# Sixteen chained score matmuls per head pair undone, and the last tile's 32-row stores on ScalarE's queue (block-sorted attention followed by a residual MLP, one core)

## The chip, the cores and the metric

One NeuronCore of a Trainium2 chip runs the whole program. The metric is the device time of one execution in microseconds (us). Beside it stands the span, from the first to the last instruction that the hardware profiler recorded. PE is TensorE, ACT ScalarE, DVE VectorE, POOL GpSimd, SP SyncE, which here only issues DMAs and waits.

## The reference, cut to what matters

```python
# sort_net (4, 8, 8, 8) -> P: five rounds of exp and normalising, one 8x8 matrix per batch and head
k_sorted = einsum('bhij,bhjcd->bhicd', P, k_blocks)      # 8 blocks of 96 tokens, 64 wide
v_sorted = einsum('bhij,bhjcd->bhicd', P, v_blocks)
scores = matmul(q_block, k_sorted_block.T) / sqrt(64)    # 96 x 96 in each block
attn = exp(scores - max); attn = attn / sum(attn)
x = matmul(attn, v_sorted)                               # 4 batches of 768 tokens x 512

# the residual MLP on x
a1 = alpha1 * x + beta1
u = x + lam * einsum('ts,bsd->btd', w_tok, a1)           # mixes tokens, 768 x 768
a2 = alpha2 * u + beta2
out = u + lam * (maximum(a2 @ w_ch1, 0) @ w_ch2)         # 512 -> 2048 -> 512
```

Inputs and output are float32; the matmuls run on fp16 and bf16 copies.

## The kernel before

Four batches go through the same stages. Per batch: the 8x8 matrices are spread to 128x128 (`mixing_matrices`, L267), V and K are mixed by blocks (`mix_v`, `mix_k`), the attention runs by head pairs (`emit_attention`, L512), and the MLP follows: `moe_a` (token mixing `tok_ps`, the sum u, its transposition), `moe_h` (L666, 512 to 2048 with Relu: `h_ps`) and `moe_ch` (L680, 2048 to 512: `ch_ps`, then two DVE operations, then the stores). The MLP of batch b-1 is written beside the attention of batch b, so that PE has `h_ps` and `ch_ps` matmuls to do while the attention waits for its exponentials.

**The attention of batches 1 to 3.** A head pair h4 (two heads on partitions 0 to 63 and 64 to 127, four pairs) has 8 blocks in two groups g of four. A group takes eight score matmuls (K = 64 rows, 96 x 96 each; the two heads alternate between the two halves of the rows), one exponential on ACT over 96 x 768 values (`et`), eight `x_ps` matmuls (96 rows, 65 columns wide: values and row sums) and, on DVE, a reciprocal and one or two multiplications into x (`x128`; `xs` for the blocks 6 and 7, which `gather` copies to the last 32 partitions afterwards). `emit_attention` asks for the scores of pair h4 ahead of the `x_ps` of pair h4-1.

**Buffers.** `sc_ps`, `x_ps`, `k_ps`, `v_ps` and `rep_ps` take turns in the pool psA with two buffers of two PSUM banks. In the steady state a buffer goes scores of pair h4+1, `x_ps` of pair h4, scores of pair h4+2: the scores are released by their exponential, the `x_ps` by the last DVE multiplication that reads it. `h_ps`, `ch_ps` and `tok_ps` use psB with four banks.

**The order.** Up to the loop of L792 the instructions of each engine keep their written order (`keep_in_program_order`, the flag `fixed`; from L766 to L791 it is taken off and put on by engine). In the loop over batches 1 to 3 the order on each engine is fixed at compile time by a planner: it takes the written order as priority, estimates what each instruction costs, and where the first in line is not yet ready by its estimate it puts a later one. On the chip each engine then runs its list in order, and an instruction that waits holds up what stands behind it.

**The chain of sixteen.** `emit_pair` (L432) draws both psA buffers of a pair, lets the first score wait for everything in `freed[b]` (the last instructions that empty a psA buffer or fill kT: the last `mix_k` copies, the last exponential or the last DVE multiplication), and ties each of the other fifteen scores behind the one before, so that the planner puts sixteen in a row. Batch 0 uses `emit_scores`, eight at a time, in a written order.

**The stores.** For each tile of 128 rows of the result `moe_ch` issues two DMAs on SP's queue, one for 96 rows (L695) and one for 32 rows of the tail (L696). The last tile of the last batch is worked in two column ranges, 384 and 128 wide, with two stores each.

Of the kernel before, what the change touches and what calls it, by code (L numbers as in the profile page):

```python
# [7 lines left out]
FT = mybir.dt.float32  # L8
# [8 lines left out]
def kernel(  # L17
# [20 lines left out]
    nc = tc.nc  # L38

    B, H, S, D = q.shape  # L40
    NB = sort_net.shape[-1]
    BLK = S // NB
# [9 lines left out]
    TAIL = 6 * BLK  # L52
# [20 lines left out]
    pe = Engine(nc.tensor)  # L73
    dve = Engine(nc.vector)
    act = Engine(nc.scalar)
# [9 lines left out]
    def psa(shape, dtype, name):  # L85
        return psA.tile(shape, dtype, name=name, tag="psA")

    def psb(shape, dtype, name):
        return psB.tile(shape, dtype, name=name, tag="psB")

    def const(shape, dtype, name):
# [5 lines left out]
        out=ident16[:], in_=ident16[:], compare_op=ALU.not_equal, fill=1.0, base=0,  # L97
# [31 lines left out]
    qT_of = {}  # L129
# [84 lines left out]
    def spin(ps, n):  # L214
        src = ident16[:].unsqueeze(1).to_broadcast([128, 4, 128])
        for _ in range(n):
            pe.matmul(ps, ident16[:], src, start=True, stop=True)
# [104 lines left out]
    kT_of = {}  # L322
# [30 lines left out]
    def mix_k(b, share=(4, 0, 4), gs=range(3)):  # L353
        raw = raw_of[(b, 0)]
        rhs = bigP[b][:].rearrange("p g i -> p (g i)")
        if b not in kT_of:
            kT_of[b] = att.tile([128, H4 * NB, BLK], F16, name="kT", tag="kT", bufs=2)
        kv_ = kT_of[b][:].rearrange("p c (par th tp) -> p th c par tp", th=2, par=2)
        for g in gs:
            kps = psa([128, 8, 128], FT, "k_ps")  # L360
            copies = []
            for tp in range(8):
                t0 = (8 * g + tp) * 128
                pe.matmul(kps[:, tp, :], raw[:, t0:t0 + 128], rhs, start=True, stop=True)
            for par in range(2):
                for h2 in range(2):
                    src = kps[par * 64:(par + 1) * 64, :, h2 * 64:(h2 + 1) * 64].rearrange(
                        "p n (th c) -> p th c n", th=2
                    )
                    dst = kv_[h2 * 64:(h2 + 1) * 64, :, :, par, 8 * g:8 * g + 8]  # L370
                    if 2 * par + h2 < share[g]:
                        ins = dve.tensor_copy(dst, src)
                    else:
                        ins = act.copy(dst, src)
                    copies.append(ins)
            freed[b] = copies

    def mix_heads(kv, h4, out, copies):

# [32 lines left out]

    x_of = {}

    def score(b, h4, blocks, sps):
        for ii, i in enumerate(blocks):
            for h2 in range(2):
                rows = slice(h2 * 64, (h2 + 1) * 64)
                yield pe.matmul(
                    sps[0:BLK, h2, ii, 0:BLK], kT_of[b][rows, h4 * NB + i, :],  # L420
                    qT_of[b][rows, h4, :, i * 16:(i + 1) * 16], start=True, stop=True,
                )

    freed = {}

    def behind(ins, others, kind):
        for other in others:
            tc.add_manual_dep(
                ins.ins, other.ins.name, mybir.DependencyInfo(kind, mybir.DependencyReason.DATA), reason="scores"
            )  # L430

    def emit_pair(b, h4):  # L432

        pair = [psa([128, 2, 4, 128], FT, "sc_ps") for _ in range(2)]
        last = None
        for g in range(2):
            for ins in score(b, h4, range(4 * g, 4 * g + 4), pair[g]):
                if last is None:
                    behind(ins, freed[b], mybir.DependencyClass.Sync)
                else:  # L440
                    behind(ins, (last,), mybir.DependencyClass.NoSync)
                last = ins
        return [emit_exp(ps, b) for ps in pair]

    def emit_scores(b, h4, g, spins=0):
        sps = psa([128, 2, 4, 128], FT, "sc_ps")
        spin(sps[:, 0, :, :].rearrange("p i x -> p (i x)"), spins)
        for _ in score(b, h4, ((0, 1, 2, 6), (3, 4, 5, 7))[g], sps):
            pass
        return emit_exp(sps)  # L450

    def emit_exp(sps, b=0):
        et = att.tile([BLK, 2, 4, BLK], F16, name="et", tag="et", bufs=4)
        freed[b] = [act.activation(
            et[:].rearrange("p a i (r kt) -> p (a i) r kt", kt=NT),
            sps[0:BLK].rearrange("p a i x -> p (a i) x")[:, :, 0:BLK].rearrange("p n (kt r) -> p n r kt", kt=NT),
            AF.Exp, scale=scale,
        )]
        return et

    def emit_pv(b, h4, ets, x128, xs):
        for g in range(2):
            xall = psa([128, 4, 256], FT, "x_ps")
            xps = xall[0:BLK]
            flat = ets[g][:].rearrange("p a i x -> p (a i x)")
            for ii in range(4):
                i = 4 * g + ii
                for h2 in range(2):
                    at = (h2 * 4 + ii) * BLK
                    rows = min(128, 8 * BLK - at)  # L470
                    pe.matmul(
                        xall[0:rows, ii, h2 * GRP:h2 * GRP + D + 1], flat[:, at:at + rows],
                        Vs[b % NV][:, (2 * h4 + h2) * NB + i, 0:D + 1],
                        start=True, stop=True,
                    )
            recip = att.tile([BLK, 4, 2], FT, name="recip", tag="recip", bufs=3)
            sums = xps[:, :, D:D + GRP + 1:GRP]
            vals = xps[:, :, 0:2 * GRP].rearrange("p i (a g) -> p i a g", a=2)[:, :, :, 0:D]
            dve.reciprocal(recip[:], sums)
            for lo, hi in ((0, 4),) if g == 0 else ((0, 2), (2, 4)):  # L480
                i = 4 * g + lo
                cols = slice(h4 * 128, (h4 + 1) * 128)
                dst = x128[0:BLK, i:i + hi - lo, cols] if i < 6 else xs[:, :, cols]
                freed[b] = [dve.tensor_tensor(
                    dst.rearrange("p i (a d) -> p i a d", d=D), vals[:, lo:hi],
                    recip[:, lo:hi].unsqueeze(3).to_broadcast([BLK, hi - lo, 2, D]), ALU.mult,
                )]

    def pv_tiles(h4, g, et, spins=0):

# [21 lines left out]
    def emit_attention(b):  # L512
        x128 = moep.tile([128, NT, C], F16, name="x128", tag="x128", bufs=2)
        xs = moep.tile([BLK, 2, C], F16, name="xs", tag="xs", bufs=1)
        x_of[b] = x128

        def gather(lo, hi):
            for a in range(3):
                dve.tensor_copy(x128[96:128, a:a + 4:3, lo:hi], xs[32 * a:32 * a + 32, :, lo:hi])

        prev = emit_pair(b, 0)
        for h4 in range(1, H4):
            cur = emit_pair(b, h4)
            emit_pv(b, h4 - 1, prev, x128, xs)
            prev = cur
            if h4 == H4 - 1:
                gather(0, 384)
        emit_pv(b, H4 - 1, prev, x128, xs)
        gather(384, C)
# [150 lines left out]
    def moe_ch(b, hf, kks=range(3)):  # L680
        hT = hT_of[(b, hf)]
        for kk in kks:
            kt = 3 * hf + kk
            last = b == B - 1 and kt == NT - 1
            ost = att.tile([128, C], FT, name="ost", tag="ost", bufs=2)
            for lo, hi in ((0, 384), (384, C)) if last else ((0, C),):
                cps = psb([128, hi - lo], FT, "ch_ps")
                for m in range(HT):
                    pe.matmul(
                        cps[:], hT[m][:, kk * 128:(kk + 1) * 128], W2p[:, m, lo:hi],  # L690
                        start=(m == 0), stop=(m == HT - 1),
                    )
                dve.tensor_tensor(cps[:], cps[:], lamB[:, lo:hi], ALU.mult)
                dve.tensor_tensor(ost[:, lo:hi], cps[:], u_of[b][kt][:, lo:hi], ALU.add)
                nc.sync.dma_start(out[b, kt * 96:(kt + 1) * 96, lo:hi], ost[0:96, lo:hi])  # L695
                nc.sync.dma_start(out[b, TAIL + kt * 32:TAIL + (kt + 1) * 32, lo:hi], ost[96:128, lo:hi])  # L696


    ets = {}
# [1 line left out]
    def sc0(h4, g, spins=0):  # L701
        ets[(h4, g)] = emit_scores(0, h4, g, spins)
# [83 lines left out]
    for kk in range(2):  # L786
        moe_ch(0, 0, (kk,))
        mix_k(1, gs=((0, 1), (2,))[kk])
        for h4 in range(2 * kk, 2 * kk + 2):
            turn_q(1, h4, dve.tensor_copy)  # L790
# [59 lines left out]
```

The softmax here doesn't subtract the row's maximum and nothing guards it: scores larger than these inputs give would overflow.

## Time and profile before

| what | us |
|---|---|
| median of 4 runs (lowest to highest) | 269.84 (269.34 to 272.49) |
| the profiled execution | 269.8 |
| its span | 268.0 |
| PE busy | 255.9 (95% of the span) |
| DVE busy | 155.7 (58%) |
| ACT busy | 126.2 (47%) |
| POOL busy | 92.5 (35%) |
| first and last score matmul of the kernel | 18.0 and 196.1 |
| exponential, 96 x 768, each of 32 | 0.806 |
| granted TensorE clock | 1.00 |

In a line of the timeline the first number is the start in us from the beginning of the span, the second the time until the last instruction of the group ends; then engine, line, operation, out<-in, shape, and xN, the number of instructions merged. A matmul's length there is its latency: matmuls overlap, so their rate is read from start to start. L65 is the line of the helper through which the four compute engines issue everything, so groups are told apart by their tiles. SPq lines are DMA issues. A bracket at the end gives the idle time of the engine before the group and what ended it.

### The profile page before, as it was taken

What the parts mean: (1) busy time and instruction counts of PE and PEld (TensorE: products, weight loads), DVE (VectorE), ACT (ScalarE), POOL (GpSimd) and SP (SyncE); (2) the same over time, 40 slices, a digit from 0 to 9 for tenths busy, and PEclk for the clock granted to TensorE, in tenths of its full rate; (3) what the DMA queues carried; (4) which work ended last, traced back from release to release, by engine and by line L of the source; (5) the groups of instructions that cost most, each with busy time, mean ns of one, the idle gap of its engine ahead of it and who ended that gap; (6) DMA issues with size and microseconds to landing.
All of it is one profiled execution on the core that took longest, in us unless ns stands there. A gap on an engine that the chain in (4) does not pass through costs nothing.

```text
span 268.0 us, 5145 instructions
## 1 busy us (share of the span) xinstructions
PE 255.9 (95%) x2048; PEld 141.3 (53%) x2059; DVE 155.7 (58%) x333; ACT 126.2 (47%) x232; POOL 92.5 (35%) x100
## 2 busy tenths in 40 slices
PE   7799999999998999999999999999999999999993
PEld 2467745565555444654565444554565445545542
DVE  5878678629648996712765966714567962042033
ACT  3376757643576131990266313980465305505600
POOL 8523689203682804209527225002407200000000
PEclk9999999999999999999999999999999999999999
DMA  6999999989999443699998343494200332012012
GB/s 79 186 208 245 207 211 206 209 207 109 194 177 160 90 80 100 157 105 102 203 194 105 61 89 90 117 91 68 71 11 2 79 78 78 2 39 78 2 39 78
DMA packets 62423, 30.88 MB, mean 115 GB/s; under 512 B 48888, under 2 KB 58112, under 8 KB 62400
## 3 DMA queue, kind: packets, MB, share of 16 engines
q0 software_dynamic: 23024, 15.60, 39.3%
q1 hardware_dynamic: 39376, 14.96, 33.7%
q8 instruction: 16, 0.26, 0.4%
q14 instruction: 7, 0.06, 0.1%
HBM read 32.78 MB, written 8.65 MB: 155 GB/s over the span
## 4 chain that ended last, share of the span: by engine, by line
PE 73%; DMA 9%; ACT 6%; DVE 5%; POOL 3%; issue 2%; POOLq 0%; ACTq 0%; DVEq 0%
PE ch_ps L65 30%; PE h_ps L65 25%; PE tok_ps L65 9%; DMA wt<-in_moe_w_tok_dram 6%; ACT et L65 3%; DMA W1p<-in_moe_w_ch_dram 3%; PE x_ps L65 3%; DVE x L65 2%; ACT kT L65 2%; PE v_ps L65 2%; PE k_ps L65 1%; PE sc_ps L65 1%; POOL qn L65 1%; POOL raw L65 1%; DVE kT L65 1%
## 5 line engine op out<-in xcount | busy, mean ns | idle before, releaser
L65 PE MATMUL h_ps<-a2T,W1p 128*128 128x384 bf16 x512 | 91.9, 326 | 0.1
L65 ACT ACTIVATE hTa<-h_ps 128x384 bf16<-128x384 f32 x96 | 45.9, 492 | 50.2 <-PE h_ps L65 49.6
L65 PE MATMUL ch_ps<-W2p,hTa 128*128 128x512 bf16 (+2 forms) x289 | 65.7, 370 | 0.6
L65 PEld LDWEIGHTS <-W1p 128*128 128x128 bf16 x512 | 47.8, 98 | 30.7 <-issue 0.6
L65 DVE TENSOR_TENSOR ch_ps<-ch_ps,lamB 128x512 f32<-128x512 f32 (+2 forms) x25 | 16.9, 676 | 62.7 <-PE ch_ps L65 60.1
L65 POOL TENSOR_SCALAR u<-b1lB,rs 128x512 f32<-128x512 f32 x18 | 28.5, 1595 | 65.4 <-DVE ost L65 57.4
L65 PEld LDWEIGHTS <-hTa 128*128 128x128 bf16 x300 | 28.7, 98 | 32.4
L65 ACT ACTIVATE et<-sc_ps 96x768 f16<-96x768 f32 x32 | 24.5, 807 | 22.4 <-PE sc_ps L65 22.4
L65 PE MATMUL tok_ps<-x,w_tokT 128*128 128x512 f16 x144 | 32.3, 379 | 1.0 <-DVE x L65 1.0
L65 POOL TENSOR_TENSOR u<-x,u 128x512 f32<-128x512 f16 x22 | 25.4, 1184 | 21.5 <-DVE x L65 20.7
L65 ACT CAST u<-u 128x512 f16<-128x512 f32 x24 | 14.8, 618 | 26.4 <-DVE u L65 26.4
L65 PE MATMUL ch_ps<-W2p,hTb 128*128 128x512 bf16 (+2 forms) x100 | 25.0, 371 | 0.0
L65 PEld LDWEIGHTS <-w_tokT 128*128 128x128 f16 x180 | 14.7, 97 | 17.2 <-issue 1.0
L65 DVE TENSOR_TENSOR tok_ps<-tok_ps,a1lB 128x512 f32<-128x512 f32 x24 | 16.5, 691 | 4.8 <-PE tok_ps L65 4.7
L65 DVE CAST kT<-k_ps 64x512 f16<-64x512 f32 x24 | 16.5, 688 | 3.3 <-PE k_ps L65 3.0
L65 DVE TENSOR_TENSOR x<-x_ps,recip 96x512 f16<-96x512 f32 (+2 forms) x32 | 17.6, 554 | 1.0
L65 DVE TENSOR_TENSOR u<-tok_ps,u 128x512 f32<-128x512 f32 x24 | 16.4, 688 | 1.7
L65 ACT ACTIVATE hTb<-h_ps 128x384 bf16<-128x384 f32 x32 | 15.3, 499 | 4.1 <-PE h_ps L65 3.7
L65 DVE TENSOR_TENSOR ost<-ch_ps,u 128x512 f32<-128x512 f32 (+2 forms) x25 | 16.6, 666 | 0.7
L65 POOL DMA_DIRECT2D qn<-in_q_dram x18 | 15.4, 875 | 4.2 <-PE q_ps L65 3.4
L65 PEld LDWEIGHTS <-et 96*128 96x128 f16 (+2 forms) x288 | 13.0, 99 | 7.1 <-issue 3.5
L65 PE MATMUL x_ps<-Vs,et 96*128 96x65 f16 (+2 forms) x288 | 14.7, 194 | 1.0 <-ACT et L65 0.8
(95 smaller groups left out, 207.5 us busy)
## 6 DMA issues: line engine op xcount, KB each, us to landing
out_dram<-ost SPq DMA_DIRECT2D x23, 192.0 KB, 2.2
raw<-in_v_dram POOLq DMA_DIRECT2D x8, 384.0 KB, 8.8
raw<-in_k_dram POOLq DMA_DIRECT2D x8, 384.0 KB, 11.0
vscr<-vA SPq DMA_DIRECT2D x6, 384.0 KB, 4.4
Vs<-vscr SPq DMA_DIRECT2D x6, 384.0 KB, 7.5
W1p<-in_moe_w_ch_dram POOLq DMA_DIRECT2D x4, 512.0 KB, 10.6
W2p<-in_moe_w_ch_dram POOLq DMA_DIRECT2D x4, 512.0 KB, 18.2
qn<-in_q_dram POOLq DMA_DIRECT2D x12, 128.0 KB, 5.0
```

What stands on the lines that cost most here:

```text
L65: ins = getattr(self.eng, name)(*args, **kwargs)
```

## The change

The chain of sixteen goes: `emit_pair`, `score`, `behind`, `emit_exp` and the record `freed` are taken out, and `emit_scores`, one group of eight, serves all four batches. Each group's scores then depend only on their operands and on their own psA buffer. The number of matmuls, exponentials and DVE operations stays. For the last tile the two 32-row stores are issued on ScalarE's queue in place of SyncE's.

```diff
@@ mix_k
-            copies = []
...
                     if 2 * par + h2 < share[g]:
-                        ins = dve.tensor_copy(dst, src)
+                        dve.tensor_copy(dst, src)
                     else:
-                        ins = act.copy(dst, src)
-                    copies.append(ins)
-            freed[b] = copies
@@ scores
-    def emit_pair(b, h4):
-
-        pair = [psa([128, 2, 4, 128], FT, "sc_ps") for _ in range(2)]
-        last = None
-        for g in range(2):
-            for ins in score(b, h4, range(4 * g, 4 * g + 4), pair[g]):
-                if last is None:
-                    behind(ins, freed[b], mybir.DependencyClass.Sync)
-                else:
-                    behind(ins, (last,), mybir.DependencyClass.NoSync)
-                last = ins
-        return [emit_exp(ps, b) for ps in pair]
...
+    def emit_scores(b, h4, g, spins=0):
+        kT = kT_of[b]
+        qT = qT_of[b]
+        blocks = ((0, 1, 2, 6), (3, 4, 5, 7))[g] if b == 0 else range(4 * g, 4 * g + 4)
+        sps = psa([128, 2, 4, 128], FT, "sc_ps")
+        spin(sps[:, 0, :, :].rearrange("p i x -> p (i x)"), spins)
         for ii, i in enumerate(blocks):
             for h2 in range(2):
                 rows = slice(h2 * 64, (h2 + 1) * 64)
-                yield pe.matmul(
-                    sps[0:BLK, h2, ii, 0:BLK], kT_of[b][rows, h4 * NB + i, :],
-                    qT_of[b][rows, h4, :, i * 16:(i + 1) * 16], start=True, stop=True,
-                )
+                pe.matmul(
+                    sps[0:BLK, h2, ii, 0:BLK], kT[rows, h4 * NB + i, :], qT[rows, h4, :, i * 16:(i + 1) * 16],
+                    start=True, stop=True,
+                )
         et = att.tile([BLK, 2, 4, BLK], F16, name="et", tag="et", bufs=4)
...
@@ emit_attention
-        prev = emit_pair(b, 0)
+        prev = [emit_scores(b, 0, g) for g in range(2)]
         for h4 in range(1, H4):
-            cur = emit_pair(b, h4)
+            cur = [emit_scores(b, h4, g) for g in range(2)]
             emit_pv(b, h4 - 1, prev, x128, xs)
@@ moe_ch
                 nc.sync.dma_start(out[b, kt * 96:(kt + 1) * 96, lo:hi], ost[0:96, lo:hi])
-                nc.sync.dma_start(out[b, TAIL + kt * 32:TAIL + (kt + 1) * 32, lo:hi], ost[96:128, lo:hi])
+                (nc.scalar if last else nc.sync).dma_start(
+                    out[b, TAIL + kt * 32:TAIL + (kt + 1) * 32, lo:hi], ost[96:128, lo:hi]
+                )
```

More of the change, by code (lines that the diff above doesn't have):

```diff
@@ L371, in mix_k @@
                     if 2 * par + h2 < share[g]:
-                        ins = dve.tensor_copy(dst, src)
+                        dve.tensor_copy(dst, src)
                     else:
-                        ins = act.copy(dst, src)
-                    copies.append(ins)
-            freed[b] = copies
+                        act.copy(dst, src)
     def mix_heads(kv, h4, out, copies):
@@ L413 @@
     x_of = {}
-    def score(b, h4, blocks, sps):
+    def emit_scores(b, h4, g, spins=0):
[4 more added lines that the diff above has]
+        spin(sps[:, 0, :, :].rearrange("p i x -> p (i x)"), spins)
         for ii, i in enumerate(blocks):
@@ L418, in score @@
                 rows = slice(h2 * 64, (h2 + 1) * 64)
-                yield pe.matmul(
-                    sps[0:BLK, h2, ii, 0:BLK], kT_of[b][rows, h4 * NB + i, :],
-                    qT_of[b][rows, h4, :, i * 16:(i + 1) * 16], start=True, stop=True,
-                )
[L424 to L429, printed above, removed]
-            )
-    def emit_pair(b, h4):
-        pair = [psa([128, 2, 4, 128], FT, "sc_ps") for _ in range(2)]
-        last = None
-        for g in range(2):
-            for ins in score(b, h4, range(4 * g, 4 * g + 4), pair[g]):
-                if last is None:
-                    behind(ins, freed[b], mybir.DependencyClass.Sync)
-                else:
-                    behind(ins, (last,), mybir.DependencyClass.NoSync)
-                last = ins
-        return [emit_exp(ps, b) for ps in pair]
[L445 to L452, printed above, removed]
+                pe.matmul(
+                    sps[0:BLK, h2, ii, 0:BLK], kT[rows, h4 * NB + i, :], qT[rows, h4, :, i * 16:(i + 1) * 16],
+                    start=True, stop=True,
+                )
         et = att.tile([BLK, 2, 4, BLK], F16, name="et", tag="et", bufs=4)
-        freed[b] = [act.activation(
+        act.activation(
             et[:].rearrange("p a i (r kt) -> p (a i) r kt", kt=NT),
@@ L457, in emit_exp @@
             AF.Exp, scale=scale,
-        )]
+        )
         return et
@@ L483, in emit_pv @@
                 dst = x128[0:BLK, i:i + hi - lo, cols] if i < 6 else xs[:, :, cols]
-                freed[b] = [dve.tensor_tensor(
+                dve.tensor_tensor(
                     dst.rearrange("p i (a d) -> p i a d", d=D), vals[:, lo:hi],
                     recip[:, lo:hi].unsqueeze(3).to_broadcast([BLK, hi - lo, 2, D]), ALU.mult,
-                )]
+                )
     def pv_tiles(h4, g, et, spins=0):
@@ L695, in moe_ch @@
                 nc.sync.dma_start(out[b, kt * 96:(kt + 1) * 96, lo:hi], ost[0:96, lo:hi])
-                nc.sync.dma_start(out[b, TAIL + kt * 32:TAIL + (kt + 1) * 32, lo:hi], ost[96:128, lo:hi])
+                (nc.scalar if last else nc.sync).dma_start(
+                    out[b, TAIL + kt * 32:TAIL + (kt + 1) * 32, lo:hi], ost[96:128, lo:hi]
+                )
     ets = {}
```

## The prediction

> **What bounds the kernel now.** I read the page's first section, then the timeline of TensorE (PE) through the three attention stages, then the timeline of all engines at the end of the span, then the DMA issues.
>
> ```profile
> span 268.0 us, 5145 instructions
> PE 255.9 (95%) x2048; PEld 141.3 (53%) x2059; DVE 155.7 (58%) x333; ACT 126.2 (47%) x232; POOL 92.5 (35%) x100
> ```
>
> PE is busy for 95% of the span, and from 41 us to 264 us its timeline has hardly a gap: whatever the change does to the time in the middle, it does by adding or removing time in PE's own queue, which runs in order. The granted clock is 1.00 in all the stretches I asked for, so no term below comes from the clock.
>
> The change touches batches 1 to 3. Their attention is woven by the planner between the MLP matmuls of the batch before (h_ps, ch_ps). This is PE in batch 3; the columns are start, length, what, count.
>
> ```profile
> 189.80 2.12 PE L65 MATMUL h_ps<-a2T,W1p 128*128 128x384 bf16 x12
> 191.85 0.56 PE L65 MATMUL sc_ps<-qT,kT 64*96 64x96 f16 x16
> 192.34 0.66 PE L65 MATMUL h_ps<-a2T,W1p 128*128 128x384 bf16 x3
> 193.19 0.41 PE L65 MATMUL x_ps<-Vs,et 96*128 96x65 f16 x8 [0.19 <-ACT et L65]
> 193.44 0.49 PE L65 MATMUL h_ps<-a2T,W1p 128*128 128x384 bf16 x2
> 193.89 0.42 PE L65 MATMUL x_ps<-Vs,et 96*128 96x65 f16 x8
> 194.14 1.63 PE L65 MATMUL h_ps<-a2T,W1p 128*128 128x384 bf16 x9
> 195.70 0.56 PE L65 MATMUL sc_ps<-qT,kT 64*96 64x96 f16 x16
> ```
>
> Four numbers come out of it. (1) An h_ps matmul takes 0.163 us from start to start: two rows not shown here, h_ps x25 at 199.81 and tok_ps at 203.88, give 4.07/25. (2) Scores have a price for coming and going. Twelve h_ps from 189.80 would let the next one start at 191.75; the scores start at 191.85: 0.10 us on entry. Sixteen scores last 0.56 us, of which 0.205 is one matmul's own length (the groups by tile), so they are (0.56-0.205)/15 = 0.024 us apart, 16 make 0.38; the next h_ps starts 0.49 us after the first score: 0.11 us on exit. A visit of sixteen is thus 0.59 us, one of eight 0.10+0.19+0.11 = 0.40 us. (3) The x_ps matmuls cost no such entry: after h_ps x3 at 197.99 they start at 198.48, just 3 x 0.163 later. (4) The two x_ps groups wait for their exponentials: h_ps x3 from 192.34 end their turn at 192.83, x_ps starts at 193.19 (0.36 us lost), and the next, 193.89 against 193.77, loses 0.12. Together 0.48 us a pair; the same spacing stands at 76 to 78, 80 to 81, 132 to 133, 137 and 197 us, so six pairs. The score run itself waits for no buffer there (195.70 is 9 x 0.163 + 0.10 after 194.14, within 0.01).
>
> The second pair of each batch (h4=1) waits for both exponentials of the first:
>
> ```profile
> 175.97 1.31 PE L65 MATMUL h_ps<-a2T,W1p 128*128 128x384 bf16 x7
> 177.46 0.56 PE L65 MATMUL sc_ps<-qT,kT 64*96 64x96 f16 x16 [0.18 <-ACT et L65]
> 177.94 1.15 PE L65 MATMUL h_ps<-a2T,W1p 128*128 128x384 bf16 x6
> ```
>
> Seven h_ps end their turn at 177.11 and the scores start at 177.46: 0.35 us, entry included.
>
> Batch 1 ends differently from 2 and 3, because its filler runs out:
>
> ```profile
> 83.45 2.28 PE L65 MATMUL h_ps<-a2T,W1p 128*128 128x384 bf16 x13
> 85.66 0.20 PE L65 MATMUL rep_ps<-P,ebh 32*128 32x64 f16 x1
> 86.12 0.62 PE L65 MATMUL tok_ps<-x,w_tokT 128*128 128x512 f16 x2 [0.26 <-DVE x L65]
> 87.50 7.50 PE L65 MATMUL tok_ps<-x,w_tokT 128*128 128x512 f16 x34 [0.76 <-DVE x L65]
> 94.84 2.75 PE L65 MATMUL ch_ps<-W2p,hTa 128*128 128x512 bf16 x11
> ```
>
> The thirteen h_ps end their turn at 85.57. Until tok_ps starts at 86.12 PE does one small matmul (0.13 us by its row at 163.59): 0.42 us lost. The 36 tok_ps take 94.84-86.12 = 8.72 us where 36 x 0.216 = 7.77 would do (0.216 from the batch 3 rows, 7.77 us for 36): 0.95 us lost, waiting for the last copies of x by VectorE (DVE). So 1.37 us of PE stand idle. In batches 2 and 3, 34 and 25 h_ps stand between the last x_ps and tok_ps, and nothing is lost.
>
> The end of the span:
>
> ```profile
> 264.13 0.32 SPq L695 DMA_DIRECT2D out_dram<-ost  x1
> 264.34 0.29 DVE L65 TENSOR_TENSOR ost<-ch_ps,u 128x128 f32<-128x128 f32 x1
> 264.50 0.42 SPq L696 DMA_DIRECT2D out_dram<-ost  x1
> 265.01 0.38 SPq L695 DMA_DIRECT2D out_dram<-ost  x1
> 265.44 0.43 SPq L696 DMA_DIRECT2D out_dram<-ost  x1
> ```
>
> ```profile
> out_dram<-ost SPq DMA_DIRECT2D x2, 48.0 KB, 1.7
> out_dram<-ost SPq DMA_DIRECT2D x1, 16.0 KB, 1.5
> ```
>
> The last addition ends at 264.63. SyncE (SP) is then still issuing the first columns' 32-row store until 264.92, and the last store is issued at 265.44; with 1.5 us to landing it lands at 266.94, and 1.1 us of closing work follow.
>
> **The change part by part.** The base is the profiled execution: a span of 268.0 us and 1.8 us around it, taken as unchanged, 269.8 in all; the median of the runs is 269.84, the same.
>
> *The tail.* The stores of the 32 rows go to ScalarE (ACT), which has had nothing since the last h_ps was evicted some 10 us earlier and has nothing behind them. SP then has one issue of 0.32 us, free at 264.45, so both last stores are issued when the sum is ready, near 264.68. With 1.7 us for the 48 KB store it lands at 266.38 in place of 266.94: -0.55 us. The trace has no store issued by ACT. Its bounds: at best the end follows the last issue, which moves from 265.44 to 264.68, -0.76; if it takes the 2.2 us of the big output stores, it lands at 266.88, -0.06. I take -0.55, since SP's row of the same size (1.5 us) is nearest.
>
> *The pair.* All 256 score matmuls and 32 exponentials of the kernel stay. What goes are the edges that held a pair's first score until both buffers were free and chained the other fifteen to it. A group of eight is now free to run when its own buffer is. For h4=1 the buffers come from the two exponentials, some 0.75 us apart (1.50 us for two); for h4=2 and 3 from VectorE's evictions of x_ps group 0 and 1 (82.05 and 82.95 us in batch 1's timeline), 0.9 us apart. In such a gap the planner has two to five h_ps to place, as it now does between the two x_ps groups, which have the same two gates. So nine pairs split. For h4=2 and 3 a split costs 2 x 0.40 - 0.59 = 0.21 us, six times: 1.26. For h4=1 the waits, which cover the entry, change from 0.35 to the 0.36 and 0.12 of the x_ps: 0.36+0.30+0.12+0.30 against 0.35+0.49, +0.24, three times: 0.72. Sum +2.0 us; bounds 0 (all stay adjacent) and, with the first pairs split too, 2.6. The first pair needs all of kT, and both its buffers are free by then; I take it as whole.
>
> *A rule weighed.* The Trainium skill, TensorEngine Tiling (Array Packing), Key Properties, says that changing the tiling mode drains the array; the scores (64 rows) lie in another mode than h_ps, and the rows agree, also in that the 96-row x_ps pay nothing. For the drain's length the skill's TensorE: Matmul & The Clock Gate, Step-by-step, has some 128 cycles, at 2.4 GHz an estimate of 0.05 us a switch; the nine splits would then cost 18 x 0.05 = 1.0 us. The trace has 0.21 us a split, and I use that.
>
> *The waits.* A freed group starts its exponential earlier, so x_ps, evictions and the next scores come earlier. Round one buffer the latency is 2.7 us (scores at 79.34, group 0 evicted at 82.05), against 3.86 us now from pair to pair (191.85 to 195.70). The planner, which thinks the exponential shorter than it is, will use that and keep its 0.48 us of error per pair. Bounds, for six pairs: gone altogether, -2.9; or two score groups each held like the first x_ps, 6 x 2 x 0.36 = +4.3. I take +0.15 (nearest the present rows, a little up as ACT has exponentials closer together among its Relus).
>
> *Batch 1.* If each of two or three pairs starts 0.9 us sooner, x is complete 1.8 us or more sooner, and the 1.37 us of idle PE are gone but for what the splits push out. Bounds -1.37 and 0; I take -1.0, since the chain's last evictions and copies stay one behind the other on VectorE. The scores of batch 0 keep their written order: nothing. Behind batch 1 PE runs on unbroken, so what is gained or lost there stays.
>
> Sum: -0.55 + 2.0 + 0.15 - 1.0 = +0.6: **270.4 us**.
>
> **The rivals.** *Faster:* the free groups give the exponentials a lead that PE doesn't overrun. The place is the two x_ps waits; half of 2.9 us is won (-1.45), all of batch 1's idle goes (-1.37): 269.8 - 0.55 + 2.0 - 1.45 - 1.37 = 268.4. For it: 2.7 against 3.86 us, and ACT is busy for only 13.39 of the 19.00 us from 68.5 to 87.5. Against: the planner fills every gap it sees, and its error in the exponential isn't touched. It decides once more than 0.24 us a pair comes off the waits. *Slower:* with buffers in shorter turns PE meets each score group's gate too early, at 0.36 us each: 269.8 - 0.55 + 2.0 - 1.0 + 4.3 = 274.5. For it: PE is in order, and what waits at its head holds all h_ps behind it. Against: the eviction gate is now met without loss. *Does not do what it says:* the planner leaves the eight and eight side by side, and only the tail moves: 269.25. Against it: the x_ps pairs, split by the same gates.
>
> **How the numbers follow.** Forecast 0.55, faster 0.22, slower 0.15, nothing but the tail 0.08. The forecast's own range is 269.4 to 271.8 (the first pairs split, or half of the batch 1 idle stays; or splits half as many). To hold 8 in 10 the range goes to the faster case and half way to the slower one: 268.4 to 273.0. A change of 1%, 2.7 us, is about what a measurement of this kernel can tell from none: over 272.5 lies most of the slower case and a sliver of the forecast, 0.13; under 267.1 only the far end of the faster case, 0.04; the rest, 0.83, is the same.
>
> **What would show it.** In PE's timeline, score runs of 8 with two to five h_ps between, nine times; entry 0.10 and exit 0.11 at each; no gap of 0.95 us before tok_ps in batch 1; about the same x_ps waits; the last ACT store issued within 0.1 us of SP's and the span's end 0.5 us nearer to the last addition. I am wrong if the scores stay in runs of 16, if single scores stand among h_ps (each would pay 0.2 us), or if waits over 0.3 us stand before most score runs.

## The result, and the profile after

The changed kernel takes 268.6 us (median of 42 runs, 268.35 to 271.8) against 270.13 us before (68 runs); the ratio is 0.994 with a 95% interval of 0.9925 to 0.9955. A second comparison, below, gives 0.9975 (0.9947 to 1.0003). Some executions of either kernel come late, up to 5.7 us above the fastest before and 3.5 us after, and in the first comparison 29 of the 68 before lie above 270.5 us but only 1 of the 42 after, which pushes the medians apart; the fastest executions differ by 0.81 us there and by 0.68 us in the second comparison. The forecast was 270.4 us, a loss of 0.6 us; it is a gain. The point of the forecast and its sign were wrong; the measured time lies in its range, near the lower end, where the rival called *faster* stood with 268.4.

The page's first section of the kernel after:

```profile
span 266.7 us, 5149 instructions
PE 257.2 (96%) x2049; PEld 141.5 (53%) x2059; DVE 154.3 (58%) x333; ACT 125.7 (47%) x232; POOL 92.5 (35%) x100
```

PE is busy 1.3 us longer in a span that is 1.3 us shorter. That fits added visits of scores and less idle time, but this sum is too rough to rest on: the changed kernel traced a second time has 257.9 us, and the run with the same order on PE and the stores back on SyncE has 258.8. The account below goes by starts.

Runs with the same order on PE repeat the middle of the program to within some hundredths of a microsecond (one exception, of 0.2 us, comes below), so I cut it at four places that every trace has: the last q_ps x24 ahead of batch 1's attention, the first ch_ps after each tok_ps x36 (the end of the token stage), the end of the last addition, and the span's end. All columns are read from PE's timeline and the last lines of the timeline of all engines.

| kernel | q_ps to tok end, batch 1 | to tok end, batch 2 | to tok end, batch 3 | to last addition | to span's end | sum | against before |
|---|---|---|---|---|---|---|---|
| before | 29.82 | 58.29 | 58.52 | 52.99 | 3.39 | 203.01 | |
| after | 28.45 | 58.78 | 58.78 | 52.99 | 3.17 | 202.17 | -0.84 |

So batch 1 gives 1.37 us, batches 2 and 3 take 0.49 and 0.26, the tail gives 0.22: 0.84 us in all, a ratio of 0.997. The profiled spans differ by 1.3 us; the missing 0.5 us is in the first 42 us (batch 0's last tok_ps x6 starts at 41.29 in place of 41.80), where the change does nothing. In the fourteen traces of this case that start lies anywhere from 41.3 to 42.4 us, whichever kernel ran, and it goes with a load: POOL's last W2p issue, which waits for a W1p load to land, starts between 31.6 and 32.8 us, and the tok_ps start 9.6 us later in twelve traces and 9.9 in the other two. It is scatter.

PE in batch 3 after the change, third and fourth pair; these answer to the lines from 189.80 to 195.70 before:

```profile
190.27 0.38 PE L65 MATMUL sc_ps<-qT,kT 64*96 64x96 f16 x8
190.58 0.50 PE L65 MATMUL h_ps<-a2T,W1p 128*128 128x384 bf16 x2
191.01 0.38 PE L65 MATMUL sc_ps<-qT,kT 64*96 64x96 f16 x8
191.32 0.34 PE L65 MATMUL h_ps<-a2T,W1p 128*128 128x384 bf16 x1
191.61 0.41 PE L65 MATMUL x_ps<-Vs,et 96*128 96x65 f16 x8
191.86 0.65 PE L65 MATMUL h_ps<-a2T,W1p 128*128 128x384 bf16 x3
192.35 0.42 PE L65 MATMUL x_ps<-Vs,et 96*128 96x65 f16 x8
192.61 0.49 PE L65 MATMUL h_ps<-a2T,W1p 128*128 128x384 bf16 x2
193.04 0.38 PE L65 MATMUL sc_ps<-qT,kT 64*96 64x96 f16 x8
193.35 0.82 PE L65 MATMUL h_ps<-a2T,W1p 128*128 128x384 bf16 x4
194.11 0.38 PE L65 MATMUL sc_ps<-qT,kT 64*96 64x96 f16 x8
194.42 0.43 PE L65 MATMUL x_ps<-Vs,et 96*128 96x65 f16 x8
194.69 0.82 PE L65 MATMUL h_ps<-a2T,W1p 128*128 128x384 bf16 x4
195.46 0.42 PE L65 MATMUL x_ps<-Vs,et 96*128 96x65 f16 x8
```

Scores come in eights, as forecast, each with its entry and exit. New is what became of the x_ps waits. Before, each pair lost 0.36 and 0.12 us. Now h_ps x1 from 191.32 ends its turn at 191.48 and x_ps starts at 191.61: 0.13. The second group, at 192.35, follows three h_ps with no loss at all; the third, at 194.42, follows scores with none; the fourth loses 0.12 (195.46 against 194.69 + 4 x 0.163). Together 0.25 us where it was 0.95.

The first pair of the batch, forecast to stay whole, does not:

```profile
173.44 0.24 PE L65 MATMUL sc_ps<-qT,kT 64*96 64x96 f16 x1
173.62 0.82 PE L65 MATMUL h_ps<-a2T,W1p 128*128 128x384 bf16 x4
174.37 0.56 PE L65 MATMUL sc_ps<-qT,kT 64*96 64x96 f16 x15
```

One score runs alone and fifteen follow 0.93 us later. By the code the lone one reads the 64 rows of kT whose copies are complete, while the next, of the other head, waits for the last copy. The prediction had named single scores among h_ps as a sign of being wrong.

Batch 1's end; these answer to the lines from 83.45 to 94.84 before:

```profile
81.13 4.23 PE L65 MATMUL h_ps<-a2T,W1p 128*128 128x384 bf16 x25
85.20 7.93 PE L65 MATMUL tok_ps<-x,w_tokT 128*128 128x512 f16 x36
```

Twenty-five h_ps are left after the last x_ps where there were thirteen, and tok_ps follows them without a gap: 85.20 is 25 x 0.163 after 81.13, and 36 tok_ps take 7.77 us in place of 8.72. VectorE's last copy of x ends at 85.31 (87.45 before). The one rep_ps that stood in the gap now comes behind ch_ps, in the second column, where it costs 0.23 us (0.10 on entry, 0.13 itself).

The end, from the timeline of all engines and the DMA issues:

```profile
263.01 0.85 SPq L667 DMA_DIRECT2D out_dram<-ost  x2
263.01 0.91 ACTq L668 DMA_DIRECT2D out_dram<-ost  x2
263.22 0.29 DVE L65 TENSOR_TENSOR ost<-ch_ps,u 128x128 f32<-128x128 f32 x1
```

```profile
out_dram<-ost ACTq DMA_DIRECT2D x1, 48.0 KB, 2.2
out_dram<-ost SPq DMA_DIRECT2D x1, 48.0 KB, 1.9
out_dram<-ost ACTq DMA_DIRECT2D x1, 16.0 KB, 2.0
```

Each pair of stores is issued at the same moment by two engines, as forecast; the last issues start at 263.54 on both, 0.03 us after the last addition, and 3.17 us after that addition the span ends. The landing is what differs: 1.9 and 2.0 us for the last two in place of 1.6 and 1.5 (the 1.7 of the page before is the median of 1.7 and 1.6).

### The profile page after: what moved, and what is told of

Same layout as the page of the kernel before. It is cut to its first block, busy times and chain, and to the rows that moved or that the text cites. A ratio compares the mean times of both kernels' runs of the same rounds, so it can differ in the third digit from the quotient of the medians.

```text
span 266.7 us, 5149 instructions
## 1 busy us (share of the span) xinstructions
PE 257.2 (96%) x2049; PEld 141.5 (53%) x2059; DVE 154.3 (58%) x333; ACT 125.7 (47%) x232; POOL 92.5 (35%) x100
## 4 chain that ended last, share of the span: by engine, by line
PE 89%; ACT 4%; DVE 4%; issue 1%; DMA 1%; DVEq 0%; ACTq 0%
PE ch_ps L65 31%; PE h_ps L65 30%; PE tok_ps L65 12%; PE x_ps L65 5%; PE sc_ps L65 4%; ACT kT L65 2%; PE v_ps L65 2%; PE k_ps L65 1%; PE q_ps L65 1%; ACT et L65 1%; DVE csum L65 1%; DVE P L65 1%; PE m_ps L65 1%; DVE rsum L65 1%; DMA P<-in_sort_net_dram 1%
## 5 line engine op out<-in xcount | busy, mean ns | idle before, releaser
L65 PE MATMUL h_ps<-a2T,W1p 128*128 128x384 bf16 x512 | 93.4, 326 | 0.1
L65 PEld LDWEIGHTS <-hTb 128*128 128x128 bf16 x100 | 9.6, 98 | 10.9
L65 PEld LDWEIGHTS <-et 96*128 96x128 f16 (+2 forms) x288 | 12.4, 99 | 4.6 <-issue 1.2
```

Source lines behind the costliest of these rows:

```text
L65: ins = getattr(self.eng, name)(*args, **kwargs)
```

## The experiments

Theory A, from the first traces: the gain is batch 1's idle time; a visit of scores costs what the forecast said; the x_ps waits shrink and pay most of that back; the tail gives 0.2 us; the early 0.5 us is scatter. Its rivals: the early 0.5 us belongs to the change, to its second DMA queue (B) or to its scores (C); or every batch gains by earlier exponentials (C2).

**The tail alone.** The kernel before with this edit only:

```diff
-                nc.sync.dma_start(out[b, TAIL + kt * 32:TAIL + (kt + 1) * 32, lo:hi], ost[96:128, lo:hi])
+                (nc.scalar if last else nc.sync).dma_start(
+                    out[b, TAIL + kt * 32:TAIL + (kt + 1) * 32, lo:hi], ost[96:128, lo:hi]
+                )
```

> Only the two 32-row stores of the last tile move to ScalarE's queue; the scores stay chained by sixteen. Theory A (the 0.51 us by which the changed kernel's trace is ahead when batch 0's second token stage begins, 41.29 against 41.80, is scatter of that one execution; the tail is worth what the span's end shows, 3.18 against 3.40 us after the last addition): 0.2 to 0.3 us faster than before, ratio 0.999, batch 1 to 3 as before with tok_ps at 86.1 and 1.37 us idle before it. Rival B (the early 0.51 us comes with the second DMA queue): 0.7 to 0.8 us faster, ratio 0.997, and the early stage again at 41.3.

**The scores alone.** The changed kernel with the stores back on SyncE:

```diff
-                (nc.scalar if last else nc.sync).dma_start(
+                nc.sync.dma_start(
```

> Only the chain of sixteen is taken out; all stores stay on SyncE. Theory A: batch 1 gains 1.1 to 1.4 us, batches 2 and 3 lose 0.25 to 0.5 each, so 0.6 to 0.9 us faster, ratio 0.997, and with the tail's 0.25 that is less than the 1.6 us measured for the whole. Rival B (the early 0.51 us belongs to the queue): the same 0.6 to 0.9. Rival C (the early 0.51 us comes with the scores): 1.1 to 1.4 us faster, ratio 0.995, early stage at 41.3.

**The split in batch 1 alone, and in batches 2 and 3 alone.** The kernel before, stores on SyncE; `emit_scores` also takes its blocks in the changed kernel's order for batches 1 to 3 (not shown):

```diff
-        prev = emit_pair(b, 0)
+        def scores(b, h4):
+            if b == 1:                      # the other kernel: if b > 1
+                return [emit_scores(b, h4, g) for g in range(2)]
+            return emit_pair(b, h4)
+
+        prev = scores(b, 0)
...
-            cur = emit_pair(b, h4)
+            cur = scores(b, h4)
```

> The chain is taken out in batch 1 alone; batches 2 and 3 keep sixteen in a row, stores on SyncE. Theory A: PE's 1.37 us of idle time before batch 1's tok_ps are gone, the one rep_ps moves behind ch_ps and costs 0.25 there: 1.0 to 1.4 us faster, ratio 0.995, better than the scores of all three batches. Rival C2 (each batch gains by its earlier exponentials): a third of the whole, 0.3 to 0.5 us, ratio 0.9985.

> The chain is taken out in batches 2 and 3 alone; batch 1 keeps it, stores on SyncE. Theory A: three or four more visits of scores per batch at 0.21 us, paid back in part by the x_ps waits (0.9 to 0.3 us): 0.2 to 0.6 us slower, ratio 1.0015. Rival C2: 0.5 to 0.9 us faster. The forecast's own term (+0.67 a batch, waits unchanged): 1.3 to 1.5 us slower, ratio 1.005.

| kernel | batch 1 | batch 2 | batch 3 | tail | sum against before | median (before) | ratio, 95% interval |
|---|---|---|---|---|---|---|---|
| tail alone | 29.82 | 58.29 | 58.51 | 3.20 | -0.20 | 269.55 (269.66) | 0.9999, 0.9962 to 1.0035 |
| scores alone | 28.45 | 58.78 | 58.78 | 3.39 | -0.62 | 269.14 (269.66) | 0.9953, 0.993 to 0.9977 |
| split in batch 1 | 28.45 | 58.52 | 58.52 | 3.39 | -1.14 | 268.43 (269.66) | 0.9938, 0.9913 to 0.9964 |
| split in batches 2, 3 | 29.82 | 58.57 | 58.78 | 3.39 | +0.54 | 270.26 (269.66) | 1.0005, 0.9978 to 1.0032 |

The columns add: 28.45 comes with the split in batch 1 and only then, 58.78 with the split in the batch concerned and 58.52 without (58.29 where rep_ps stands in batch 1's gap), the tail's 0.2 with the stores. B and C fall with the early stage, which started at 42.05, 41.81, 41.35 and 41.35 us in these four. C2 falls with the fourth kernel: batches 2 and 3 lose. Medians move by -0.11, -0.52, -1.23 and +0.60 us, as the sums do; the ratios' intervals are too wide to part 0.2 us from nothing, so the tail's gain rests on the traces alone.

**Filling batch 1's gap without splitting anything.** The kernel before, with one tile of ch_ps written ahead of the token stage:

```diff
+        if b == 1:
+            moe_ch(b - 1, 1, (0,))
         moe_a(b)
-        moe_ch(b - 1, 1)
+        moe_ch(b - 1, 1, range(1, 3) if b == 1 else range(3))
```

> The kernel before with its chain of sixteen everywhere and all stores on SyncE; in batch 1 alone one tile of the second half's ch_ps (16 matmuls, 3.45 us) is written ahead of the token stage. Theory A (the gain of the change is batch 1's idle PE, 1.37 us, and nothing of the earlier exponentials): the gap before tok_ps is filled and 1.2 to 1.4 us are won without splitting anything, ratio 0.9955. Rival C2 (the gain comes from the scores' earlier start): at most 0.2 us, ratio 1.000, or slower, as x is used 2 us later and batch 1's transposes with it.

> As the one before, with the last tile's 32-row stores on ScalarE. Theory A, stages adding: 1.4 to 1.6 us faster than before, ratio 0.9945, and 0.6 us faster than the changed kernel. Rival C2: at most 0.4 us, ratio 0.9985.

Both fell short of the 1.2 to 1.6 us expected: 269.3 us, ratio 0.9972 (0.9944 to 1.0), and with the tail 269.03 us, 0.9972 (0.9947 to 0.9997), against 269.59 before. The sums of the stages give -0.48 and -0.46. The first step came true. PE of the first of the two:

```profile
85.53 2.75 PE L65 MATMUL ch_ps<-W2p,hTa 128*128 128x512 bf16 x12
88.12 1.03 PE L65 MATMUL ch_ps<-W2p,hTb 128*128 128x512 bf16 x4
88.99 7.93 PE L65 MATMUL tok_ps<-x,w_tokT 128*128 128x512 f16 x36
...
103.89 2.45 PE L65 MATMUL h_ps<-a2T,W1p 128*128 128x384 bf16 x14
106.98 1.04 PE L65 MATMUL v_ps<-raw,bigV 128*128 128x512 f16 x4 [0.63 <-DVE bigV L65]
```

The sixteen ch_ps fill the gap and tok_ps runs through; batch 1's stage is 31.76 us, 3.45 of them the moved tile, so 28.31 against 29.82. But 0.80 us of the 1.51 are lost again: fourteen h_ps from 103.89 end their turn at 106.16 and v_ps starts at 106.98. It waits for bigV, and VectorE's timeline says why bigV is late:

```profile
103.68 1.25 DVE L65 TENSOR_SCALAR a2T<-a2T,ab2col 128x384 bf16<-128x384 f16 x4 [1.85 <-DMA a2T<-u]
104.85 0.69 DVE L65 TENSOR_TENSOR ch_ps<-ch_ps,lamB 128x512 f32<-128x512 f32 x1
105.45 0.21 DVE L65 TENSOR_TENSOR sel<-rep_ps,mskj 128x64 f32<-128x64 f32 x1
105.58 0.69 DVE L65 TENSOR_TENSOR ost<-ch_ps,u 128x512 f32<-128x512 f32 x1
106.18 0.21 DVE L65 TENSOR_REDUCE red<-sel 128x8 f32<-128x64 f32 x1
106.42 0.29 DVE L65 TENSOR_TENSOR bigP<-mskb,red 128x128 f16<-128x128 f16 x1
106.63 0.28 DVE L65 TENSOR_TENSOR bigV<-mskv,red 128x128 f16<-128x128 f16 x1
```

VectorE takes its list in order. Its a2T stands first and waits 1.85 us for its transposes. In the kernel before it waited as long (1.87 us), but there 48 ch_ps lay between tok_ps and the next h_ps; now only 32 do, and sel, red and bigV wait behind it, though sel's input rep_ps was done at 103.96. In the second of the two kernels a2T waits 2.06 us and batch 2's stage is 0.21 us longer than in the first, so the tail's 0.2 us doesn't show in its sum. The stall went from before tok_ps to before v_ps. So idle time before tok_ps is confirmed as worth 1.4 to 1.5 us, and the split of batch 1 is the better way to fill it: x is ready sooner, and behind its ch_ps only the moved rep_ps is to be paid (0.23 us).

**The first pair held together.** The changed kernel; `filled[b]` keeps the four copies of the last `mix_k` part:

```diff
+                if b > 0 and h4 == 0 and g == 0 and ii == 0 and h2 == 0:
+                    for other in filled[b]:
+                        tc.add_manual_dep(
+                            ins.ins, other.ins.name,
+                            mybir.DependencyInfo(mybir.DependencyClass.Sync, mybir.DependencyReason.DATA), reason="scores"
+                        )
```

> The changed kernel, but the first score of each batch's first pair waits for all four copies of the last kT part, so that it doesn't run alone ahead of the other fifteen. Theory A (every visit of scores costs about 0.21 us in coming and going, and PE has no idle time to hide it): 0.2 to 0.25 us a batch less than the changed kernel, 1.4 to 1.6 us faster than before, ratio 0.9945; the scores of the first pairs in one run of 16. Rival (the lone score only fills time in which PE would wait for kT): no difference to the changed kernel, ratio 0.997 by its stages.

268.08 us, ratio 0.993 (0.9904 to 0.9956); stages 28.24, 58.50 and 58.51: a visit saved in each batch, 0.21, 0.28 and 0.27 us. The scores of the first pairs now stand in one run of sixteen, which bears out the reading of the lone score, and the price of coming and going is measured by itself. With it, splitting costs batches 2 and 3 nothing (58.50 and 58.51 against 58.52 with all sixteens).

The split in batch 1 with the tail's edit, all other pairs chained, asks whether the parts add:

> The chain is taken out in batch 1 alone and the last tile's 32-row stores go to ScalarE. Theory A, in which the stages simply add: batch 1 -1.37, the moved rep_ps +0.23, tail -0.20: 1.3 us faster than before, ratio 0.995, and 0.5 us faster than the changed kernel. Rival (the parts don't add, the tail has nothing of its own as in the run with the tail alone): 1.1 us, ratio 0.996.

268.03 us, ratio 0.9939 (0.9905 to 0.9973); sum -1.37, which is the -1.14 of the split in batch 1 and the -0.22 of the changed kernel's tail. They add.

**Which pairs pay the split back.** Both on top of the kernel with the first pairs held, with `filled[b]` also taking the last exponential or VectorE multiplication:

```diff
-                if b > 0 and h4 == 0 and g == 0 and ii == 0 and h2 == 0:
+                if b > 0 and (h4 == 0 or (b > 1 and h4 == 1)) and g == 0 and ii == 0 and h2 == 0:
                 # the other kernel: b > 1 and h4 > 1
```

> The changed kernel with the first pairs held together and, in batches 2 and 3, also the second pair (h4=1): its first score waits for both exponentials of the first pair. Nothing there hurries, since the x_ps that follow come only behind 48 ch_ps. Theory A (a split costs its visit unless an x_ps wait pays it back, and at h4=1 none does): 0.15 to 0.2 us a batch less than with the first pairs alone held, stage of batch 3 at 58.33 in place of 58.51, 1.9 us faster than before in all, ratio 0.993. Rival (what pays the splits back is spread over all pairs): no gain, 58.5 or more.

> The changed kernel with the first pairs held together and, in batches 2 and 3, also the third and fourth (h4=2, 3); h4=1 stays split. Theory A (at h4=2 and 3 the split takes away 0.2 to 0.3 us of x_ps waits a pair, somewhat more than the visit costs): the x_ps waits of 0.36 and 0.12 come back, stage of batch 3 at 58.65 to 58.75 in place of 58.51, 0.3 to 0.5 us slower over both batches than with the first pairs alone held. The forecast's reading (waits don't change with the split): 0.2 us a split won, stage at 58.1, 0.8 us faster.

With h4=1 held, 267.71 us, ratio 0.9931 (0.9901 to 0.9961), stages 58.33 and 58.33: 0.17 and 0.18 us won. PE in batch 3:

```profile
174.23 1.31 PE L65 MATMUL h_ps<-a2T,W1p 128*128 128x384 bf16 x7
175.72 0.56 PE L65 MATMUL sc_ps<-qT,kT 64*96 64x96 f16 x16 [0.17 <-ACT et L65]
176.21 1.15 PE L65 MATMUL h_ps<-a2T,W1p 128*128 128x384 bf16 x6
```

This is again the picture of before, seven h_ps and sixteen scores after a 0.35 us wait. With h4=2 and 3 held, 268.51 us, ratio 0.9949 (0.992 to 0.9979), stages 58.70 and 58.71: 0.20 us lost in each. PE in batch 3:

```profile
191.23 0.66 PE L65 MATMUL h_ps<-a2T,W1p 128*128 128x384 bf16 x3
192.08 0.41 PE L65 MATMUL x_ps<-Vs,et 96*128 96x65 f16 x8 [0.19 <-ACT et L65]
192.33 0.49 PE L65 MATMUL h_ps<-a2T,W1p 128*128 128x384 bf16 x2
192.78 0.41 PE L65 MATMUL x_ps<-Vs,et 96*128 96x65 f16 x8
```

The two waits are back: 192.08 against 191.23 + 0.49, and 192.78 against 192.33 + 0.33. So at h4=2 and 3 a split pays for itself and 0.10 us more a pair, by the waits; at h4=1, where no x_ps follows closely, it costs 0.17. Theory A had put the two stages at 58.33 and at 58.65 to 58.75; the forecast's reading had 58.1 for the second.

**The very last store alone on ScalarE.** The kernel with the first pairs held:

```diff
-                (nc.scalar if last else nc.sync).dma_start(
+                (nc.scalar if last and lo else nc.sync).dma_start(
```

> The changed kernel with the first pairs held together; of the last tile's stores only the very last (16 KB, the second column range) is on ScalarE, the first range's 32 rows are back on SyncE. Crowding theory (ScalarE's packets come late because four stores are handed to the same 16 engines at once): the ScalarE store lands 1.5 to 1.7 us after its issue, and SyncE's 48 KB store, issued some 0.37 us after the last addition, ends the span: 3.05 us after the addition. Queue theory (a store on ScalarE's queue beside SyncE's takes 2.0 to 2.2 us by itself): 2.0 us to land, span's end 3.15 to 3.2 us after the addition, as with both.

267.9 us, ratio 0.9909 (0.9871 to 0.9948; 9 runs); against the kernel with the first pairs held, whose median in an earlier comparison is 268.08, no difference that these timings can tell. The end:

```profile
262.97 0.29 DVE L65 TENSOR_TENSOR ost<-ch_ps,u 128x128 f32<-128x128 f32 x1
263.13 0.42 SPq L677 DMA_DIRECT2D out_dram<-ost  x1
263.30 0.38 ACTq L677 DMA_DIRECT2D out_dram<-ost  x1
263.64 0.38 SPq L676 DMA_DIRECT2D out_dram<-ost  x1
```

The span ends 3.10 us after the addition (3.18 with both stores on ScalarE, 3.39 with none). ScalarE's store lands 1.80 us after its issue, where it took 2.0 to 2.1 us as the second of two on its queue and 1.5 us as the last of four on SyncE's. That lies between the theories: with one store less on its queue ScalarE's store lands 0.2 us sooner, but it stays 0.3 us slower than the last of four in one queue. What makes it so stays open.

**The changed kernel again.**

> The changed kernel once more, without an edit. If its traces' stages are the whole of it (batch 1 -1.37, batch 2 +0.49, batch 3 +0.26, tail -0.21), it is 0.8 us faster than before, ratio 0.997; if the first comparison's 1.6 us is the truth, ratio 0.994 and some 0.7 us stands outside the stages, in the first 42 us. The early stage anywhere from 41.3 to 42.1, stages to within 0.02 us of the first trace.

268.75 us against 269.64, ratio 0.9975 (0.9947 to 1.0003), stages 28.45, 58.78, 58.78, tail 3.23. The median moves by 0.89 us, the stages by 0.78. The first comparison's median of before (270.13) is half a microsecond above those of the three later ones (269.59 to 269.66). I take 0.7 to 0.9 us as the change's effect, from the stages, the fastest executions and this second median; why the first median of before lies higher stays open.

## Why the prediction was wrong

By its own terms, in us; the measured ones are summed from gaps between starts in PE's timeline, before against after.

| term | forecast | measured | where |
|---|---|---|---|
| tail | -0.55 | -0.22 | span's end |
| visits of scores | +2.0 | +2.65 | 0.88, 0.80, 0.97 in batches 1 to 3 |
| x_ps waits | +0.15 | -1.96 | -0.72, -0.56, -0.68 |
| batch 1's idle time | -1.0 | -1.29 | -1.52 there (1.37 idle and rep_ps's own turn), +0.23 for the moved rep_ps |
| sum | +0.6 | -0.82 | -0.84 by the stages |

How much of a gap goes to the visits and how much to the waits is a choice in places, worth about 0.1 us a batch between the two rows; their sum is held by the stages.

**The waits: the step that failed.** The prediction said that the planner "will use that and keep its 0.48 us of error per pair" and took +0.15 out of a range from -2.9 to +4.3. The traces show 0.12 to 0.18 us a pair in place of 0.48 (batch 2's two pairs had lost 0.41 before, where the prediction counted 0.48 for all six). ScalarE's exponentials of the third and fourth pair of batch 3, before (the third alone) and after:

```profile
192.34 1.50 ACT L65 ACTIVATE et<-sc_ps 96x768 f16<-96x768 f32 x2
```

```profile
190.76 1.53 ACT L65 ACTIVATE et<-sc_ps 96x768 f16<-96x768 f32 x2
193.52 0.81 ACT L65 ACTIVATE et<-sc_ps 96x768 f16<-96x768 f32 x1
194.60 0.81 ACT L65 ACTIVATE et<-sc_ps 96x768 f16<-96x768 f32 x1
```

The first exponential doesn't start any sooner behind its scores: 0.49 us after the first of them before (192.34 against 191.85), 0.49 and 0.48 after (190.76 against 190.27, 193.52 against 193.04). The first x_ps follow that first score after 1.34 us before and after 1.34 and 1.38 us now. What has changed is PE's own work in that time. With the pair whole it has sixteen scores and three h_ps, 0.98 us, and stands for 0.36. With the pair split, the second group's scores and the h_ps ahead of them come in between: from 190.27 to 191.48 in the third pair, with 0.13 us left to wait, and from 193.04 to 194.42 in the fourth, without a gap. The second groups come there by VectorE's evictions of x_ps, as the prediction had it:

```profile
192.30 0.69 DVE L65 TENSOR_TENSOR x<-x_ps,recip 96x512 f16<-96x512 f32 x1
193.48 0.41 DVE L65 TENSOR_TENSOR xs<-x_ps,recip 96x256 f16<-96x256 f32 x1
```

They end at 192.99 and 193.89, and the two groups of scores start at 193.04 and 194.11. So the reason given was half right: waits of 0.12 to 0.18 us remain, but most of what held PE is now covered by PE's own work. The run with h4=2 and 3 held brings the waits back, the one with h4=1 held loses nothing: the cause is shown at the pairs where it acts. That the planner's estimate of the exponential is too short was argued from the gaps and not tested by itself.

**Visits of scores.** The price was right: 0.21 us a split, and the first pairs measured 0.21 to 0.28 by themselves (a split at h4=1 measured 0.17 where 0.24 had been put). Mis-sized was their number. "I take it as whole" was wrong for the first pair: a dependency on part of kT lets one score go ahead. That is 0.76 us over three batches, and the upper bound of 2.6 was the truth. The rule of the Trainium skill that speaks against the change (TensorEngine Tiling (Array Packing), Key Properties: a change of tiling mode drains the array) agrees with every run here, in that each visit of scores pays on entry and on exit; the drain itself no trace shows. The drain of some 128 cycles in TensorE: Matmul & The Clock Gate, Step-by-step, an estimate of 0.05 us a switch, is half of what entry (0.10) and exit (0.11) cost.

**Batch 1.** Right in kind and a little too cautious: all 1.37 us went.

**The tail.** The issue times came out as forecast; the landing did not. The rows of 1.5 and 1.7 us came from stores issued one after the other by one engine, 0.37 to 0.51 us apart. Two pairs handed over at once take 1.9 to 2.2 us each. The skill's DMA: Bandwidth & Descriptors, Issuing engines are not separate DMA queues, says that issuing from several engines saves the sequencer's time only. The traces agree, and most of the saved time is lost again: behind the last addition, the last issue starts 0.78 us earlier (0.03 us after it in place of 0.81), its landing takes 0.50 us longer, the closing work 0.06, and the span ends 0.22 earlier.

Of the rivals the one called *faster* had the place and the point of decision right: 0.33 us a pair came off the waits (1.96 over six pairs) where 0.24 were needed. Its reason, a lead of the exponentials, is not what the rows show: they start no sooner behind their scores. That its 268.4 us is 0.2 from the measured median is in part luck: it had visits of 2.0 for 2.65, waits of -1.45 for -1.96 and a tail of -0.55 for -0.22, and the change it gave, 1.4 us, is more than the 0.8 of the stages. It was given 0.22 because the prediction looked at which errors the planner makes and not at which work would stand in front of them.

## What to carry to other kernels

Before pricing a wait of an in-order engine after a change, lay the new order out by hand for one period and ask what work of that engine will stand between the producer and the wait; a wait that is planned too short costs only what nothing covers. A split that costs an engine time pays where it takes a longer wait off the same engine or where the stage runs out of filler, and costs where neither is so: the best kernel here keeps the first pairs whole, splits all others in batch 1, and in batches 2 and 3 splits only the third and fourth pair (267.71 us against 269.64 before and 268.75 for the change as it was made). Idle time that is filled with work from later can reappear as a wait there.

## What the runs showed of the hardware that was not expected

A store issued by ScalarE at the same moment as one by SyncE lands later though it is a third of the size: 2.2 against 2.0 us for the first pair (48 and 144 KB), 2.0 against 1.9 us for the last (16 and 48 KB). In the trace's packets, those of ScalarE's first store begin 1.3 us after its issue, those of SyncE's 0.8 us; with only the very last store on ScalarE its packets begin 1.0 us after the issue. A matmul of 64 rows between two of 128 rows costs 0.21 to 0.28 us in entry and exit even when it is a single one (the lone first score), some ten times its share of 0.024 us in a run of sixteen.
